# Sigmoid attention and gated layers on one core: half loads of the first group, four value loads per batch, another first pass

## The chip, the cores and the metric

The kernel runs on one core of a Trainium2 chip. A core has TensorE (matrix products into PSUM), VectorE, ScalarE, GpSimd and SyncE, each with its own instruction queue, worked off in order, and 16 DMA engines that all queues share. The metric is the time of one execution on the device, in microseconds; lower is better.

## The reference

The inputs are q, k, v of shape 8 x 12 x 448 x 64 (batches, heads, positions, width), two weights and a vector beta.

```python
scores = scale * np.matmul(q, k.transpose(0, 1, 3, 2)) - np.log(S)
attn = 1.0 / (1.0 + np.exp(-scores))
x = np.matmul(attn, v)                 # per head; then heads side by side: 3584 x 768
h = x @ w_in                           # 3584 x 2048
out = (h * (1.0 / (1.0 + np.exp(-beta * h)))) @ w_out    # 3584 x 768
```

There is no row sum in this attention, so a block of scores is finished after one sigmoid.

## The kernel before, in words

All matrix products are in fp16. A *group* is four heads of a batch, so a batch has three groups and there are 24 in all; a *pair* is two heads of a group. The tile `raws[g]` holds k and q of a group with 32 partitions per head: partition p of a head has positions 14p to 14p + 13, so that a load reads long rows. `transpose` turns them on VectorE in blocks of 32 x 32 into `kT` and `qT`, 32 partitions per head, whose two elements per position are the two halves of the head's width of 64.

`score` is one matmul with 32 rows: one head, one half of the width (`e`). Four heads of a group lie in four row groups of TensorE's array, and the loops put matmuls of different row groups next to each other. Keys are cut in four blocks: three of 128 and a last one of 64 (`KL`), of which two heads or pairs share a tile. Scores go into *score tiles* of two PSUM banks; in the first pass there are three of them (`share_psum(3)`), later two. `weigh` is ScalarE's sigmoid from a score tile into a slot of `attns`. `half_visit(g, c0, second)` makes the scores of a whole group for half of the queries (224): with `second` 0 the key blocks 0 and 1, with 1 the blocks 2 and the last. It takes two score tiles and gives two sigmoids, 128 x 896 each, or one of 896 and one of 448.

`attend` multiplies the weighted scores with v (432 matmuls on L340 in all) into one PSUM bank per pair, and VectorE casts the result to `xTs`. The values of a batch lie in `vs[b]`: block i of 32 partitions holds, per head, three key rows (`j` 0 to 2) and, in a fourth place (`JF`), the last 64 keys, which `double_v_last` copies from the lower 64 partitions to the upper on VectorE. `load_v_full` fills the first three places with four loads, `load_v_last` the fourth with two loads of short rows.

`dense1` is the first layer for a column block `dc` of 128 (six matmuls, then a sigmoid on ScalarE, L374, and a product on VectorE, L377); column blocks 2i and 2i + 1 need the w_in load `(2i, 2i + 2)`. Dense work is a list of *units* (one matmul each) that is poured between other work. Later batches use products with fewer multiplications (L531, L651), which the diff doesn't touch.

The order on each engine is the order of the code (a manual schedule). Loads into fp16 from fp32 are issued by GpSimd, in the order of `LOADS` for the start and `LATER` after it. The first group alone is loaded as fp32 by SyncE into `staged` and cast by ScalarE (`act` true, L806) and VectorE (L808). Then `BEGIN`, a list written by hand, gives the order of the first pass, that of batch 0: casts, transposes (`k`, `q` with a half of the queries), scores (`scores`, L237 and L250), values (`values`, L340), the copies of the last keys (`v`), dense units and `idle` matmuls on a tile of zeros (L822). An entry stands in the queue of whichever engines work on it, and an engine waits at its own part of it. After `BEGIN` come 74 *visits* (numbered from 0), each the scores of a group for one key block over all queries, with dense units behind it; how many follows from the work left over the visits left, and the tables `MORE` and `LATE` correct it by visit number.

Of the kernel before, what the change touches and what calls it, by code (L numbers as in the profile page):

```python
# [8 lines left out]
FP32 = mybir.dt.float32  # L9
FP16 = mybir.dt.float16  # L10
# [3 lines left out]
def kernel(  # L14
# [10 lines left out]
    nc = tc.nc  # L25
# [3 lines left out]
    B, H, S, D = q.shape  # L29
# [9 lines left out]
    NF = JF * P // BLK  # L39
# [103 lines left out]
    def load_v_full(b: int, lo: int = 0, hi: int = H):  # L143
# [4 lines left out]
        for i in range(HQ):  # L148
            nc.gpsimd.dma_start(
                out=vs[b][i * BLK : (i + 1) * BLK, lo:hi, 0:JF].rearrange("p h j d -> p h (j d)"),  # L150
                in_=rows[:, :, JF * i * D : JF * (i + 1) * D],
            )
            ready.update((b, "full", t, i) for t in range(lo // HQ, hi // HQ))

    def load_v_last(b: int):
        if b not in vs:
            vs[b] = vp.tile([P, H, JF + 1, D], FP16, tag="v16", name="v16")
        rows = v[b].rearrange("h (p c) d -> p h c d", c=NB)
        for c in range(NF, NB):
            lo = (c - NF) * BLK  # L160
            nc.gpsimd.dma_start(out=vs[b][lo : lo + BLK, :, JF], in_=rows[:, :, c])
        ready.add((b, "last"))

    def load_v(b: int):
        load_v_full(b)
        load_v_last(b)

    def double_v_last(b: int):
        assert (b, "last") in ready
        ready.add((b, "v"))  # L170
        nc.vector.tensor_copy(out=vs[b][KL:P, :, JF], in_=vs[b][0:KL, :, JF])
# [29 lines left out]
    def transpose(g: int, r: int, c0: int = 0, c1: int = NB):  # L201
        raw = raws[g][:, r]
        assert g or (r, c0) == (0, NB // 2) or all((r, "cast", c) in ready for c in range(c0, c1))
        if r == 0:
            if g not in qT:
                qT[g] = qTp.tile([P, NB * BLK, PAIR], FP16, tag="qT", name="qT")
            ready.update((g, "q", c) for c in range(c0, c1, NB // 2))
            nc.vector.transpose(
                out=in_order(g // QPB, qT[g][:, c0 * BLK : c1 * BLK]),
# [3 lines left out]
        ready.add((g, "k"))  # L213
        kT[g] = kTp.tile([P, S, PAIR], FP16, tag="kT", name="kT")
        to = kT[g].rearrange("p k e -> p (k e)").bitcast(FP32)
# [813 lines left out]
```

## Time and profile before

| | us |
|---|---|
| median of 3 runs (373.41 to 374.0) | 373.94 |
| profiled execution | 374.6 |
| its span | 372.8 |
| TensorE busy in it | 365.8 (98%) |
| ScalarE busy | 259.9 (70%) |
| VectorE busy | 254.5 (68%) |
| GpSimd busy | 90.6 (24%) |

In the rows of the profile PE is TensorE, PEld its weight loads, ACT ScalarE, DVE VectorE, POOL GpSimd; L340 is line 340 of the kernel. A row of a timeline gives start, length, engine, line, operation, output and inputs, shapes and how many, and in brackets the idle time of that engine just before it and what ended it. Matmuls of a few instructions are merged in one row; ends of matmuls are modelled. The granted clock is 1.00 in all parts of the span.

### The profile page before, as it was taken

The numbers are of one execution on the slowest core, as the hardware profiler recorded it, in microseconds if no ns is written. First come the engines' busy times: TensorE is split into PE (matmuls) and PEld (weight loads), VectorE is DVE, ScalarE is ACT, GpSimd is POOL, SyncE is SP. The second block draws the span as 40 slices with busy tenths as digits, with TensorE's granted clock in tenths as the row PEclk, the third lists the DMA queues.
The fourth block names the chain that finished last, engine by engine and source line by source line (L and its number), as shares of the span: only waits on it lengthen the run. The fifth ranks groups of instructions, "written<-read, shape, count | busy, mean of one in ns | idle before, by whom it ended". The sixth has DMA issues, their size and how long they took to land.

```text
span 372.8 us, 7320 instructions
## 1 busy us (share of the span) xinstructions
PE 365.8 (98%) x2906; PEld 184.4 (49%) x2906; DVE 254.5 (68%) x479; ACT 259.9 (70%) x311; POOL 90.6 (24%) x136
## 2 busy tenths in 40 slices
PE   7989999999999999999999999999999999999997
PEld 4566644443444455544444445554444455555655
DVE  3435696877496966787667666778667666669671
ACT  5995777699876658887777749887787647883000
POOL 6833253151151012325123003235100002230000
PEclk9999999999999999999999999999999999999999
DMA  9999999993359030039829511018903111000334
GB/s 162 165 189 202 197 203 201 245 125 51 49 76 183 2 86 1 0 51 125 157 42 206 108 26 33 3 17 116 172 6 86 42 44 42 1 2 1 86 84 128
DMA packets 42626, 34.65 MB, mean 93 GB/s; under 512 B 21968, under 2 KB 39008, under 8 KB 42592
## 3 DMA queue, kind: packets, MB, share of 16 engines
q0 software_dynamic: 36688, 22.47, 44.5%
q1 hardware_dynamic: 5904, 11.71, 11.1%
q8 instruction: 23, 0.38, 0.4%
q14 instruction: 11, 0.09, 0.1%
HBM read 45.62 MB, written 11.01 MB: 152 GB/s over the span
## 4 chain that ended last, share of the span: by engine, by line
PE 92%; ACT 5%; issue 1%; DMA 1%; DVE 1%; ACTq 0%
PE ps L651 27%; PE ps L531 26%; PE ps L237 11%; PE ps L340 10%; PE ps L362 9%; PE ps L392 4%; PE ps L445 4%; ACT attns L250 3%; DMA gt<-in_k_dram 1%; ACT attns L265 1%; ACT sg L374 1%; DVE gt L377 0%; DVE kT L217 0%; ACT raw L806 0%; ACT osb L672 0%
## 5 line engine op out<-in xcount | busy, mean ns | idle before, releaser
L265 ACT ACTIVATE attns<-ps,nlogs 128x1792 f16<-128x1792 f32 x75 | 131.6, 1755 | 41.7 <-PE ps L237 41.6
L651 PEld LDWEIGHTS <-sum 128*128 128x128 f16 x440 | 40.5, 98 | 37.3 <-issue 12.5
L545 POOL TENSOR_TENSOR gt<-attns,sg 128x448 f16<-128x448 f32 x21 | 23.9, 1139 | 141.7 <-ACT sg L542 141.7
L237 PE MATMUL ps<-qT,kT 32*128 32x448 f16 (+3 forms) x864 | 52.1, 339 | 1.2 <-ACT attns L250 0.4
L542 ACT ACTIVATE sg<-ps,beta_sb 128x448 f32<-128x448 f32 x72 | 45.2, 632 | 8.4 <-PE ps L531 5.9
L531 PE MATMUL ps<-xT,w_in 128*128 128x448 f16 x216 | 49.2, 353 | 0.0
L531 PE MATMUL ps<-xT,w_S 128*128 128x448 f16 x216 | 49.2, 352 | 0.0
L651 PE MATMUL ps<-w_T,sum 128*128 128x384 f16 x264 | 48.7, 327 | 0.0
L545 DVE TENSOR_TENSOR gt<-ps,sg 128x448 f16<-128x448 f32 x72 | 44.3, 618 | 4.0 <-ACT sg L542 3.8
L349 DVE CAST xT<-ps 128x448 f16<-128x448 f32 (+1 forms) x54 | 28.8, 567 | 21.0 <-PE ps L340 21.0
L531 PEld LDWEIGHTS <-w_in 128*128 128x128 f16 x288 | 28.0, 98 | 26.6 <-issue 0.7
L362 PE MATMUL ps<-xT,w_in 128*128 128x448 f16 (+1 forms) x240 | 39.9, 316 | 1.2 <-DMA w_in<-in_moe_w_in_dram 0.6
L340 PE MATMUL ps<-attns,v 128*64 128x448 f16 (+3 forms) x432 | 40.4, 340 | 0.6 <-issue 0.6
L669 DVE TENSOR_TENSOR osb<-ps,osb 128x384 f32<-128x384 f32 x55 | 30.5, 554 | 15.1 <-PE ps L651 12.8
L638 DVE TENSOR_TENSOR sum<-gt 128x1024 f16<-128x1024 f16 x55 | 36.5, 678 | 0.2
L377 DVE TENSOR_TENSOR gt<-ps,sg 128x448 f16<-128x448 f32 (+1 forms) x40 | 20.1, 527 | 23.2 <-ACT sg L374 23.1
L126 POOL DMA_DIRECT2D raw<-in_q_dram x26 | 14.5, 559 | 79.6 <-DVE kT L221 72.6
L651 PE MATMUL ps<-w_out,gt 128*128 128x384 f16 x176 | 33.3, 327 | 0.0
L651 PE MATMUL ps<-w_out,sum 128*128 128x384 f16 x176 | 32.3, 327 | 0.0
L591 DVE TENSOR_TENSOR ps<-ps,attns 128x448 f32<-128x448 f32 x24 | 15.2, 632 | 23.3 <-PE ps L531 19.3
L362 PEld LDWEIGHTS <-w_in 128*128 128x128 f16 x240 | 21.8, 98 | 18.0 <-issue 5.4
L531 PEld LDWEIGHTS <-w_S 128*128 128x128 f16 x216 | 21.1, 98 | 19.4
(54 smaller groups left out, 376.4 us busy)
## 6 DMA issues: line engine op xcount, KB each, us to landing
out_dram<-osb SPq DMA_DIRECT2D x100, 96.0 KB, 2.1
raw<-in_k_dram POOLq DMA_DIRECT2D x23, 224.0 KB, 5.5
raw<-in_q_dram POOLq DMA_DIRECT2D x21, 224.0 KB, 3.9
v<-in_v_dram POOLq DMA_DIRECT2D x32, 144.0 KB, 6.2
w_in<-in_moe_w_in_dram POOLq DMA_DIRECT2D x8, 384.0 KB, 11.8
w_out<-in_moe_w_out_dram POOLq DMA_DIRECT2D x4, 768.0 KB, 13.4
v<-in_v_dram POOLq DMA_DIRECT2D x16, 48.0 KB, 6.1
out_dram<-osb SPq DMA_DIRECT2D x5, 144.0 KB, 2.4
```

Of the source, the lines that this page charges most:

```text
L237: nc.tensor.matmul(sco[base : base + nk, hh, u0 : u0 + n], kT[g][lo : lo + BLK, jt * P : jt * P + nk, e], qT[g][lo : lo + BLK, c0 : c0 + n ...
L265: nc.scalar.activation(out=attns[:, slot : slot + 2].rearrange("p n h s -> p (n h) s"), in_=sco, func=AF.Sigmoid, bias=nlogs[:, 0:1], scal ...
L340: nc.tensor.matmul(av[hh * D : (hh + 1) * D, 0:n], vs[b][base : base + nk, 2 * (s % NPAIR) + hh, jt], at[base : base + nk, hh, 0:n], start ...
L349: nc.vector.tensor_copy(out=xTs[b][:, s % NPAIR, c0 : c0 + n], in_=av[:, 0:n])
L362: nc.tensor.matmul(m1, w_in16[:, hc, dc * P : (dc + 1) * P], xTs[b][:, hc, c0 : c0 + n], start=(hc == 0), stop=(hc == NHC - 1),)
L377: nc.vector.tensor_tensor(out=gt[:, dc, off : off + n], in0=m1, in1=sg[:, 0:n], op=ALU.mult)
L531: nc.tensor.matmul(out, w[:, c, i * P : (i + 1) * P], m[:, c], start=(start and c == 0), stop=(c == KH - 1), skip_group_check=not start,)
L542: nc.scalar.activation(out=sg, in_=h, func=AF.Sigmoid, bias=0.0, scale=beta_sb[:, dc : dc + 1])
L545: return lambda: engine.tensor_tensor(out=gt[:, dc, b % 2 * S : b % 2 * S + S], in0=h, in1=sg, op=ALU.mult)
L638: nc.vector.tensor_tensor(out=sums[t, i], in0=x, in1=y, op=op)
L651: nc.tensor.matmul(m2, (x if op is None else sums[t, i])[:, dc], w[:, dc], start=first, stop=(dc == ND - 1), skip_group_check=i >= 4,)
L669: nc.vector.tensor_tensor(out=out, in0=in0, in1=in1, op=op)
```

## The change

The first group's loads of k and q are cut by pairs of heads: four loads of 64 partitions instead of two of 128, and casts and transposes for each pair. A new `pair_visit` makes the scores of one pair for key blocks 0 and 1: one score tile, one sigmoid of 128 x 896. In `BEGIN` it stands for four of the half visits. The keys are dealt to the blocks differently, so that the last 64 keys belong to blocks 0 and 1 (`rows_of`: these hold four key rows per partition, blocks 2 and 3 three). A batch's values then come in four loads, two of them with rows a third longer, and the two loads of short rows fall away; `transpose` of k is cut in 256 and 192 columns instead of 384 and 64. Batch 0's values are loaded as those of group 0, ahead of group 2's q, and the rest after it; the copy of the last keys is cut likewise. Two memsets move from GpSimd to VectorE. `BEGIN` and two entries of `MORE` are new.

```diff
-    def load_v_full(b: int, lo: int = 0, hi: int = H):
+    def rows_of(i: int):
+        n = JF + int(i < KL // BLK)
+        return i * JF + min(i, KL // BLK), n
+
+    def load_v(b: int, lo: int = 0, hi: int = H):
...
         for i in range(HQ):
+            c, n = rows_of(i)
             nc.gpsimd.dma_start(
-                out=vs[b][i * BLK : (i + 1) * BLK, lo:hi, 0:JF].rearrange("p h j d -> p h (j d)"),
-                in_=rows[:, :, JF * i * D : JF * (i + 1) * D],
+                out=vs[b][i * BLK : (i + 1) * BLK, lo:hi, 0:n].rearrange("p h j d -> p h (j d)"),
+                in_=rows[:, :, c * D : (c + n) * D],
             )
-    def load_v_last(b: int):
...
-    def double_v_last(b: int):
-        nc.vector.tensor_copy(out=vs[b][KL:P, :, JF], in_=vs[b][0:KL, :, JF])
+    def double_v_last(b: int, lo: int = 0, hi: int = QPB):
+        heads = slice(lo * HQ, hi * HQ)
+        nc.vector.tensor_copy(out=vs[b][KL:P, heads, JF], in_=vs[b][0:KL, heads, JF])
...
-        nc.vector.transpose(
-            out=to[:, 0 : JF * P].rearrange("p (j i q) -> p i j q", j=JF, i=HQ),
-            in_=frm[:, 0:NF].rearrange("p (i j) f -> p i j f", j=JF),
-        )
-        nc.vector.transpose(
-            out=to[:, JF * P :], in_=frm[:, NF:].rearrange("p c f -> p (c f)")
-        )
+        half = to.rearrange("p (x i q) -> p x i q", i=2, q=BLK)
+        for i in (0, 2):
+            c, n = rows_of(i)
+            nc.vector.transpose(
+                out=half[:, i // 2 :: 2].rearrange("p j i q -> p i j q"),
+                in_=frm[:, c : c + 2 * n].rearrange("p (i j) f -> p i j f", j=n),
+            )
...
+    def pair_visit(g: int, c0: int, x: int):
+        s, sco = 2 * g + x, score_tile()
+        for jt in (0, 1):
+            for e in range(PAIR):
+                for hh in range(2):
+                    score(sco, jt * QH, s, jt, hh, e, c0, QH)
+        slot = weigh(sco, S)
...
         LOADS = [
-            ("q", 1, 0), ("k", 1), ("k", 2), ("last",), ("q", 2, 0), ("v", 0, 3), ("q", 1, 1), ("q", 0, 1),
-            ("q", 2, 1), ("w_in", 0, 2), ("w_in", 2, 4), ("w_in", 4, 6), ("w_in", 6, 8), ("w_in", 8, 10),
+            ("q", 1, 0), ("k", 1), ("k", 2), ("v", 0, 1), ("q", 2, 0), ("v", 1, 3), ("q", 0, 1), ("q", 2, 1),
+            ("q", 1, 1), ("w_in", 0, 2), ("w_in", 2, 4), ("w_in", 4, 6), ("w_in", 6, 8), ("w_in", 8, 10),
...
-        for r, (to, n) in parts.items():
-            nc.sync.dma_start(
-                out=to[:, 0 : n * D],
-                in_=(q, k)[r][0, 0:HQ].rearrange("h (p c) d -> (h p) (c d)", c=NB)[:, 0 : n * D],
-            )
+        for x in (0, 1):
+            rows = slice(x * 2 * BLK, (x + 1) * 2 * BLK)
+            for r, (to, n) in parts.items():
+                nc.sync.dma_start(
+                    out=to[rows, 0 : n * D],
+                    in_=(q, k)[r][0, 2 * x : 2 * (x + 1)].rearrange("h (p c) d -> (h p) (c d)", c=NB)[:, 0 : n * D],
+                )
...
-        nc.gpsimd.memset(nlogs, NEG_LOG_S)
-        nc.gpsimd.memset(dummy, 0.0)
...
+        nc.vector.memset(dummy, 0.0)
+        nc.vector.memset(nlogs, NEG_LOG_S)
...
         BEGIN = [
-            ("cast", 1, 0, 8, False), ("cast", 1, 8, 14, True), ("cast", 0, 0, 7, True), ("k", 0), ("q", 0, 0),
-            ("q", 1, 0), ("idle", 20), ("scores", 0, 0, 1), ("idle", 4), ("scores", 0, 0, 0), ("k", 1),
-            ("idle", 2), ("k", 2), ("q", 2, 0), ("idle", 2), ("scores", 1, 0, 0), ("beta",), ("idle", 8),
-            ("scores", 1, 0, 1), ("v", 0), ("idle", 6), ("scores", 2, 0, 0), ("values", 0, 0), ("q", 1, 1),
-            ("scores", 2, 0, 1), ("q", 0, 1), ("values", 1, 0), ("scores", 0, 1, 0),
-            ("values", 2, 0), ("scores", 0, 1, 1), ("dense", 12), ("scores", 1, 1, 1), ("two",), ("dense", 6),
-            ("scores", 1, 1, 0), ("loads",), ("q", 2, 1), ("dense", 21), ("scores", 2, 1, 0), ("dense", 9),
-            ("values", 0, 1), ("scores", 2, 1, 1), ("values", 1, 1), ("values", 2, 1), ("dense", 39), ("k", 3),
-            ("q", 3, 0), ("q", 3, 1), ("dense", 45),
+            ("cast", 1, 0, 0, 9, False), ("cast", 1, 0, 9, 14, True), ("cast", 0, 0, 0, 7, True), ("k", 0, 0),
+            ("q", 0, 0, 0), ("cast", 1, 1, 0, 7, False), ("cast", 1, 1, 7, 14, True),
+            ("cast", 0, 1, 0, 7, True), ("k", 0, 1), ("q", 0, 0, 1), ("idle", 17), ("pair", 0, 0, 0),
+            ("q", 1, 0), ("scores", 0, 0, 1), ("pair", 0, 0, 1), ("idle", 4), ("k", 1), ("idle", 2), ("k", 2),
+            ("v", 0, 1), ("q", 2, 0), ("pair", 1, 0, 0), ("pair", 1, 0, 1), ("idle", 2), ("values", 0, 0),
+            ("beta",), ("scores", 1, 0, 1), ("idle", 2), ("pair", 2, 0, 0), ("pair", 2, 0, 1), ("v", 1, 3),
+            ("q", 0, 1), ("q", 1, 1), ("values", 1, 0), ("scores", 2, 0, 1), ("pair", 0, 1, 0),
+            ("pair", 0, 1, 1), ("values", 2, 0), ("scores", 0, 1, 1), ("dense", 12), ("scores", 1, 1, 1),
+            ("two",), ("dense", 6), ("scores", 1, 1, 0), ("loads",), ("q", 2, 1), ("dense", 21),
+            ("scores", 2, 1, 0), ("dense", 9), ("values", 0, 1), ("scores", 2, 1, 1), ("values", 1, 1),
+            ("values", 2, 1), ("dense", 33), ("k", 3), ("q", 3, 1), ("q", 3, 0), ("dense", 45),
         ]
...
         MORE = {
-            0: -1, 2: 1, 3: -4, 8: -3, 9: 1, 10: 1, 12: 2, 13: 1, 14: -2, 15: 1, 16: -1, 17: -2, 19: -1, 20: -2,
+            0: -1, 2: 2, 3: -3, 8: -3, 9: 1, 10: 1, 12: 2, 13: 1, 14: -2, 15: 1, 16: -1, 17: -2, 19: -1, 20: -2,
...
-            54: 1, 59: 1, 62: 1, 67: -1,
+            54: 1, 59: 1, 62: 1, 67: -1, 80: 2, 82: 1,
```

More of the change, by code (lines that the diff above doesn't have):

```diff
@@ L232, in score @@
         g, lo = s // 2, (s % 2 * 2 + hh) * BLK
[L233 to L234 removed]
+        assert (g, "k", s % 2) in ready and all(
+            (g, "q", c, s % 2) in ready for c in range(c0 // BLK, (c0 + n) // BLK, NB // 2)
         )
```

64 lines of the change are left out of this document (28 added, 36 removed).

## The prediction

> **What bounds the kernel now.** I read the windows by stage first, then ScalarE's, TensorE's and the weight loads' timelines of the first 31 us, and last GpSimd's timeline with each load's time to landing. In the windows (columns: window and its length; busy time and instructions of TensorE, weight loads, VectorE, ScalarE, GpSimd; clock; DMA share; GB/s) TensorE is full from 31.2 us on. What the change rewrites lies ahead of that:
>
> ```profile
> 6.00:16.00 10.00, 8.68 (x142) 4.91 (x143) 4.23 (x14) 8.82 (x11) 7.12 (x12) 1.00 1.35 169
> 16.00:31.20 15.20, 13.91 (x222) 9.30 (x216) 6.35 (x19) 13.86 (x20) 6.53 (x9) 1.00 1.41 186
> 31.20:44.00 12.80, 12.80 (x92) 8.18 (x92) 8.00 (x19) 7.01 (x14) 3.00 (x5) 1.00 1.33 202
> 44.00:74.00 30.00, 30.00 (x272) 13.69 (x265) 23.15 (x40) 21.45 (x15) 11.40 (x19) 1.00 1.29 215
> ```
>
> Much of TensorE's time before 31 us is idle matmuls and waiting; ScalarE is the full engine there. Its timeline (start, length, then the idle before it) shows the first sigmoid of the scores at 6.70, and hardly a gap from there to 24:
>
> ```profile
> 4.35 1.10 ACT L806 CAST raw<-gt 128x384 f16<-128x384 f32 x2 [2.11 <-DMA gt<-in_k_dram]
> 6.70 8.68 ACT L250 ACTIVATE attns<-ps,nlogs 128x896 f16<-128x896 f32 x10 [1.25 <-PE ps L237]
> 15.75 4.99 ACT L250 ACTIVATE attns<-ps,nlogs 128x896 f16<-128x896 f32 x6 [0.37 <-PE ps L237]
> 23.04 1.79 ACT L265 ACTIVATE attns<-ps,nlogs 128x1792 f16<-128x1792 f32 x1
> 26.62 1.75 ACT L265 ACTIVATE attns<-ps,nlogs 128x1792 f16<-128x1792 f32 x1 [0.57 <-PE ps L237]
> ```
>
> The weight loads of TensorE, one engine further on, show what the whole start waits for: at 14.05 the values, and at 24.24 and 25.59 the third and fourth load of w_in.
>
> ```profile
> 14.05 0.55 PEld L340 LDWEIGHTS <-v 128*64 128x64 f16 x12 [0.80 <-DMA v<-in_v_dram]
> ...
> 24.24 1.07 PEld L362 LDWEIGHTS <-w_in 128*128 128x128 f16 x12 [0.87 <-DMA w_in<-in_moe_w_in_dram]
> 25.59 0.21 PEld L362 LDWEIGHTS <-w_in 128*128 128x128 f16 x3 [0.28 <-DMA w_in<-in_moe_w_in_dram]
> ```
>
> Issue plus time to landing gives the loads in microseconds from the start: k of group 1 8.3, k of group 2 9.5, the two `last` loads of v 10.5 and 10.8, group 2's q 11.3, the four big v loads 11.7 to 14.0 (0.75 apart), the late halves of q 14.6 to 15.7, then w_in 18.9, 21.0, 24.2, 25.55. GpSimd issues all of these:
>
> ```profile
> 8.56 0.61 POOL L149 DMA_DIRECT2D v<-in_v_dram  x1 [1.19 <-DMA raw<-in_k_dram]
> 9.80 0.56 POOL L126 DMA_DIRECT2D raw<-in_q_dram  x1 [0.63 <-DMA raw<-in_k_dram]
> 10.78 1.07 POOL L126 DMA_DIRECT2D raw<-in_q_dram  x2 [0.42 <-DMA v<-in_v_dram]
> 11.84 6.59 POOL L177 DMA_DIRECT2D w_in<-in_moe_w_in_dram  x8
> ```
>
> From the ninth on, each issue waits for the landing of the load eight before it.
>
> **The change, step by step.** Times are starts from the profiled execution, 374.6 us (span 372.8, 1.8 around it); the median of the runs is 373.94, 0.66 lower, and I take the same difference off both.
>
> *First score.* All of k lands at 4.32, q's half at 4.86. Half the rows land somewhere between half of k's 3.58 us after 0.74 (2.5) and no earlier than now (4.3); I take 3.2 for k and 3.6 for q, nearer to the early end because 448 KB and 224 KB are moved one after the other now, and 4.5 and 4.9 for the second half, whose last byte cannot come earlier. Casts: no row has a cast over 64 partitions; it costs between half and all of one over 128, and I take all, since an engine goes through the columns. So by 0.51 us for 384 columns and 0.57 for 448, ScalarE's four cost 0.43 + 3 x 0.57 instead of 1.08, one microsecond more. VectorE's cast (0.48), kT's two transposes (0.50 + 0.13 now for 448 columns; 0.64 for 256 + 192) and qT (0.37) follow the first landing to 4.8; the 17 idle matmuls end at 4.95 (20 take 4.45). So the first pair's scores begin near 4.95 instead of 5.94. ScalarE must first do the second half's casts, queued ahead of its sigmoid: 4.52, 5.07, then the first sigmoid at 5.6 instead of 6.70. Gain 1.1.
>
> *Where that goes.* The second half's transposes end at 6.2, the next scores need all four heads (0.75 to the sigmoid, as 5.94 to 6.70 now), so the second sigmoid stands at 7.0 and ScalarE idles 0.5. Group 0's first half is then done by 9.3 (0.91 per sigmoid, 0.52 for a narrow one); k of group 1 lands at 8.3, its transposes take 0.64, a pair's scores about 0.55: next sigmoid 9.6 instead of 10.1. Gain 0.45. No row shows a pair's eight matmuls, which use two row groups and not four. Bounds: 0.35 (half of sixteen) and 0.8 (the slower sixteen, 0.75); I take 0.55, near the fast sixteen's 0.51. At 0.8 the start still ends with its wait for w_in; only at 1.0 would the start be longer than now, by 0.8.
>
> *Values earlier.* `values` of group 0 moves ahead of the scores of (1, 0, 1) on TensorE's queue. Its four small loads follow k of group 2 (9.5). They are a third of 4 x 0.75 = 3.0, plus the bytes of `last`, so 1.2: landed at 10.7. TensorE waits 0.3, runs 0.92, and the scores behind it reach ScalarE at 12.4 instead of 11.9: it idles about one microsecond. Loss 0.5. It is given back where `values` stood (the gap before 15.75, and 0.16 after each narrow sigmoid, which a pair's single score tile removes): (2, 0, 1) at 15.7 instead of 15.75, the first two-tile sigmoid at 22.8 instead of 23.04. ScalarE's chain is thus 0.2 ahead, and without any wait for weights TensorE would reach the last `values` of the start 0.86 earlier than now. The second value load (two groups) and its copy, 0.42 now and 0.2 + 0.3 after in two pieces, lie on VectorE, 42% busy there.
>
> *The weights.* Dense columns 4 to 7 need the third and fourth w_in loads, and nothing behind them in TensorE's order is changed until the visits. So the gain of the start is what the fourth landing (25.55) gains, at most 0.86. Bytes ahead of it are the same. GpSimd loses two memsets: 0.07 (they start 0.035 apart) to 0.55 (0.74 to 1.29, when the first load is issued), and I take 0.07, as the 0.42 behind them are not theirs. The two `last` loads bring 96 KB in 1.29 us; in the big loads' pace, 144 KB in 0.75, these bytes need 0.50, so 0 to 0.79 are saved; I take 0.25, as the queue is seldom held up by one kind of load. Against it, fifteen loads and not thirteen stand before w_in on GpSimd at about 0.6 each: with the same eight-load wait, I get the first w_in issue at 12.65 instead of 11.84, a cost of 0 (the q loads ahead of it land until 15) to 0.8; I take 0, since w_in lands 7.1 us after its issue, most of it queueing. Sum: 0.07 + 0.25 = 0.3 earlier; ends 1.3 earlier (of which 0.86 count) and 0.8 later.
>
> The Trainium skill, "DMA: Bandwidth & Descriptors", section Specifications, says that an element below 512 B costs a read-modify-write. By that rule the loads that now bring 512 B a row would run faster than the old 384 B and the gain would be the whole 0.86. The trace disagrees for 384 B: 144 KB per 0.75 us is the pace of w_in's 512 B pieces (384 KB per 2.0 us); only the 128 B pieces of `last` are slower.
>
> *After 31 us.* Six dense units move from ahead of the first visit into the visits; TensorE is full on both sides, so 0, with 0.3 either way for the order. Every k is transposed in 256 + 192 columns instead of 384 + 64: same elements, same count, 0. Two value loads less per batch are 1.3 us of GpSimd (24% busy) per batch: 0; were GpSimd late, the next k and q would gain. The entries 80 and 82 of the unit table have no visit (74 there are): 0.
>
> Sum: -0.3, so 374.3 for a profiled execution, 373.6 for the median.
>
> **Rivals.** A difference within 0.2% (0.75 us) can hardly be told from none.
> (1) *The fourth w_in load pins the start*, as above: 373.6, its own range 373.2 to 374.4. Speaking for it: the 0.87 and 0.28 waits. If half loads land no earlier than whole ones, the change doesn't do what it says at 4.95, yet this case stays, because k of group 1 and the values bind next.
> (2) *The weights come early enough*, 0.8 or more: the start ends when ScalarE lets it, 0.86 earlier, 373.1; with 0.3 from the order of the visits 372.8. For it: the slow 128 B loads vanish. Against: bytes are the same, and w_in's own pace of 2.0 us does not change.
> (3) *The weights come later*, slower: two more issues ahead of w_in push its first issue by 0.8; as soon as the fourth lands after 25.55, each further microsecond is one on the span: 374.7 at the full 0.8. For it: GpSimd is 71% busy from 6 to 16 us. Against: 7.1 us from issue to landing. The values' wait can't do this before they land 0.9 late.
>
> **Numbers.** Case 1 has 0.48, case 2 0.27, case 3 0.25 (it includes visits that fit worse by some 0.5 after the move). These are also the chances of same, faster, slower. Prediction 373.6. The range takes in most of cases 2 and 3: 372.7 to 375.0.
>
> **What would show it.** First sigmoid near 5.6; a ScalarE gap of about 1 us before 12.4; `values` near 10.75; weight loads still waiting for w_in around 25.3; span up to 31 us shorter by 0.3. Wrong, if no weight load waits for w_in (case 2), if the fourth w_in lands after 25.55 (case 3), if a pair's scores take 1.0, or if TensorE shows new gaps after 40 us.

## The result, and the profile after

The changed kernel takes 378.42 us (median of 6 runs, 377.52 to 380.64) where the kernel before takes 373.97 (6 runs beside them, 373.41 to 374.69): 1.0126 times as long, 95% interval 1.0098 to 1.0155. The prediction was 373.6 with a range to 375.0, so the result lies outside it, and the loss is 4.5 us.

The profiled execution took 378.47 us, its span is 376.7, 3.9 above the 372.8 of before. The windows of the changed kernel, cut as before (window and length; busy time of TensorE, weight loads, VectorE, ScalarE, GpSimd; clock; DMA share; GB/s):

```profile
6.00:16.00 10.00, 6.32 (x68) 3.51 (x67) 4.03 (x12) 5.98 (x8) 6.58 (x11) 0.66 1.10 150
16.00:31.20 15.20, 13.85 (x224) 9.34 (x222) 6.41 (x20) 14.54 (x21) 7.93 (x11) 1.00 1.39 186
31.20:44.00 12.80, 12.65 (x126) 8.15 (x121) 7.93 (x21) 7.81 (x14) 2.96 (x6) 1.00 1.31 203
44.00:74.00 30.00, 30.00 (x262) 14.67 (x259) 21.79 (x38) 21.51 (x18) 9.11 (x15) 1.00 1.18 192
```

Between 6 and 16 us ScalarE does 5.98 us of work where it did 8.82, and the granted clock of TensorE, 1.00 before, is 0.66. Everything from 31 us on is the work of before, moved by a constant: the last block of TensorE starts at 368.31 instead of 364.82, 3.49 later, and the two-tile sigmoids in between are 3.36 to 3.49 later all the way from 56 us. Another 0.4 came with the landing of the last stores. So the loss was made in the first 31 us.

ScalarE's timeline of the changed kernel shows where (start, length, engine and line, and in brackets the idle time just before, with what ended it):

```profile
4.32 0.46 ACT L815 CAST raw<-gt 64x320 f16<-64x320 f32 x1 [2.09 <-DMA gt<-in_k_dram]
5.17 0.56 ACT L815 CAST raw<-gt 64x448 f16<-64x448 f32 x1 [0.39 <-DMA gt<-in_q_dram]
8.44 0.56 ACT L815 CAST raw<-gt 64x448 f16<-64x448 f32 x1 [2.71 <-DMA gt<-in_k_dram]
9.30 0.56 ACT L815 CAST raw<-gt 64x448 f16<-64x448 f32 x1 [0.29 <-DMA gt<-in_q_dram]
9.88 1.01 ACT L247 ACTIVATE attns<-ps,nlogs 128x896 f16<-128x896 f32 x1
...
17.14 8.06 ACT L247 ACTIVATE attns<-ps,nlogs 128x896 f16<-128x896 f32 x10 [0.66 <-PE ps L234]
```

The first half of k is there at 4.3, no earlier than all of k before (4.32), the first half of q at 5.14, later than q before (4.86). The second halves land at 8.4 and 9.3. The first sigmoid, at 6.70 before, starts at 9.88 behind their casts. TensorE's timeline has the same hole, 3.46 us without a matmul:

```profile
6.22 0.67 PE L234 MATMUL ps<-qT,kT 32*128 32x224 f16 x10 [1.22 <-DVE qT L204]
10.35 1.93 PE L234 MATMUL ps<-qT,kT 32*128 32x224 f16 x22 [3.46 <-DVE qT L204]
```

SyncE issues the four halves one after the other, 0.57 to 0.60 us each (before: 0.38 and 0.42), so the last is issued at 2.62, while GpSimd has issued loads since 1.24. The chain that ended last begins with exactly this load:

```profile
2.62 6.65 DMA gt<-in_q_dram
9.28 0.02 issue
9.30 0.57 ACT raw L815
9.87 0.02 issue
9.89 0.42 DVE qT L204
10.31 0.04 issue
10.35 1.93 PE ps L234 x21
```

GpSimd's timeline of the changed kernel, to be held against the one shown in the prediction:

```profile
9.38 0.58 POOL L154 DMA_DIRECT2D v<-in_v_dram  x1 [2.82 <-DMA raw<-in_k_dram]
10.55 1.15 POOL L154 DMA_DIRECT2D v<-in_v_dram  x2 [0.60 <-DMA raw<-in_k_dram]
11.69 1.65 POOL L125 DMA_DIRECT2D raw<-in_q_dram  x3
13.31 0.86 POOL L171 DMA_DIRECT2D w_in<-in_moe_w_in_dram  x1
```

Its wait for k of group 1 is 2.82 instead of 1.19, and the first w_in load is issued at 13.31 instead of 11.84; yet no weight load of TensorE waits for w_in any more, since everything ahead of it is later still.

### The profile page after: what moved, and what is told of

It is laid out like the page before. It is cut to its first block, busy times and chain, and to the rows that moved or that the text cites. A ratio compares the mean times of both kernels' runs of the same rounds, so it can differ in the third digit from the quotient of the medians.

```text
span 376.7 us, 7285 instructions
## 1 busy us (share of the span) xinstructions
PE 366.0 (97%) x2891; PEld 184.6 (49%) x2891; DVE 256.3 (68%) x486; ACT 260.6 (69%) x313; POOL 82.9 (22%) x122
## 4 chain that ended last, share of the span: by engine, by line
PE 91%; ACT 5%; DMA 2%; issue 1%; SPq 0%; DVE 0%; ACTq 0%
PE ps L659 27%; PE ps L539 25%; PE ps L234 11%; PE ps L348 10%; PE ps L370 9%; PE ps L400 4%; PE ps L453 4%; ACT attns L247 3%; DMA gt<-in_q_dram 2%; ACT attns L262 1%; ACT sg L382 1%; PE ps L831 1%; SPq L805 0%; DVE gt L385 0%; ACT raw L815 0%
## 5 line engine op out<-in xcount | busy, mean ns | idle before, releaser
L234 PE MATMUL ps<-qT,kT 32*128 32x448 f16 (+3 forms) x864 | 53.4, 344 | 5.6 <-DVE qT L204 4.7
L539 PEld LDWEIGHTS <-w_in 128*128 128x128 f16 x288 | 28.0, 98 | 26.6 <-issue 0.7
L234 PEld LDWEIGHTS <-kT 32*128 32x128 f16 (+1 forms) x864 | 15.6, 97 | 33.8 <-issue 28.1
```

What stands on the lines that cost most here:

```text
L234: nc.tensor.matmul(sco[base : base + nk, hh, u0 : u0 + n], kT[g][lo : lo + BLK, jt * P : jt * P + nk, e], qT[g][lo : lo + BLK, c0 : c0 + n ...
L539: nc.tensor.matmul(out, w[:, c, i * P : (i + 1) * P], m[:, c], start=(start and c == 0), stop=(c == KH - 1), skip_group_check=not start,)
```

## Experiments on the half loads

All times below are medians; each interval is the ratio to runs of the kernel before on the same chip (373.2 to 373.7 there).

**The half loads undone, and the half loads alone.** The first kernel is the changed one with two whole loads by SyncE; casts and transposes stay by pairs.

```diff
-        for x in (0, 1):
-            rows = slice(x * 2 * BLK, (x + 1) * 2 * BLK)
-            for r, (to, n) in parts.items():
-                nc.sync.dma_start(
-                    out=to[rows, 0 : n * D],
-                    in_=(q, k)[r][0, 2 * x : 2 * (x + 1)].rearrange("h (p c) d -> (h p) (c d)", c=NB)[:, 0 : n * D],
-                )
+        for r, (to, n) in parts.items():
+            nc.sync.dma_start(
+                out=to[:, 0 : n * D],
+                in_=(q, k)[r][0, 0:HQ].rearrange("h (p c) d -> (h p) (c d)", c=NB)[:, 0 : n * D],
+            )
```

> The changed kernel with the first group's k and q loaded whole again (two loads of 128 partitions); casts, transposes, pairs, values and order stay as changed. Theory A (the second half loads arrive late, at 8.4 and 9.3 us, because four short loads begin later and then share the DMA engines with GpSimd's loads; all of the 3.5 us lost up to 31 us comes from there): k lands near 4.3, q near 4.9, first sigmoid near 6.5, no long TensorE gap, clock 1.00, 373.4 to 374.3. Theory B (pairs on two row groups and the new order of the first pass cost the time): still above 376.5.

Measured: 374.93, ratio 1.0036 (1.0020 to 1.0052), between the ranges of the two theories and nearer to the first. The second kernel is the one before, with only its two loads cut in four (the same diff the other way round, on that kernel):

> The kernel before with only the first group's k and q loads cut in half loads, in the changed kernel's order; its casts still need both halves. Theory A: the last half of k lands near 8.4, the last half of q near 9.3, the first sigmoid moves from 6.7 to about 11, and the time rises by about 4 to 378. Theory B: within 0.75 of before.

Measured: 378.86, ratio 1.0139 (1.0120 to 1.0157), the whole loss and a little more; the first sigmoid there is at 10.99. The second halves of k and q land at 6.8 and 8.8 there, earlier than in the changed kernel, whose GpSimd issues other loads behind k of group 2. So the half loads are worth 3.5 us in the changed kernel (378.42 less 374.93), and what is left with whole loads stands some 1.2 behind the kernel before. The two prices don't add: the cut alone cost 5.1 us.

**Why the second half is late.** In one kernel the second halves are issued by ScalarE, so that they don't stand behind the first ones in SyncE's queue.

```diff
-                nc.sync.dma_start(
+                (nc.sync, nc.scalar)[x].dma_start(
```

> The changed kernel with the second pair's two half loads issued from ScalarE's queue instead of SyncE's. If the second halves are late because they are issued third and fourth on one queue (0.62 apart) and start only when the queue gets to them: they land before 6, first sigmoid near 6.5, time 373.6 to 375. If they are late because GpSimd's loads take the DMA engines from 3 us on, whoever issues: they land at 7 or later and the time stays above 377.

Measured: 376.55, ratio 1.0076 (1.0061 to 1.0091). All halves land by 6.9 us, and the first sigmoid starts at 8.16; this lies between the two cases that were expected. In another, GpSimd's loads are held back:

```diff
+        hold = const.tile([P, 128], FP32, name="hold")
+        for _ in range(14):
+            nc.gpsimd.memset(hold, 0.0)
         for x in LOADS:
             load(*x)
```

> The changed kernel, with fourteen memsets of a scratch tile on GpSimd ahead of its first load, so that its loads start some 2 us later. Theory A1, sharing: the second halves are late because GpSimd's k of groups 1 and 2 move at the same time; then they land here at about 5.8 (k) and 6.9 (q) instead of 8.4 and 9.3, although everything of GpSimd lands 1 to 2 us later, and the time is within 1 us of the changed kernel. Theory A2, a half load is slow by itself (64 partitions use part of the engines): k still lands at 7.5 or later and the time is 379.5 or more.

Measured: 377.20 (376.50 to 380.18), ratio 1.0113 (1.0083 to 1.0143). GpSimd's first load was issued at 4.28 instead of 1.24. ScalarE's timeline of this kernel:

```profile
4.19 1.13 ACT L815 CAST raw<-gt 64x320 f16<-64x320 f32 x2 [1.96 <-DMA gt<-in_k_dram]
5.83 1.13 ACT L815 CAST raw<-gt 64x448 f16<-64x448 f32 x2 [0.51 <-DMA gt<-in_k_dram]
6.98 1.01 ACT L247 ACTIVATE attns<-ps,nlogs 128x896 f16<-128x896 f32 x1
```

The casts of the second half start at 5.83 instead of 8.44 (8.23 and 8.48 in two kernels further on with the same loads), with the same four issues by SyncE at the same times. So of the lateness of the second k, 2.6 us is the sharing of the DMA engines with GpSimd's loads, which were issued before it; without that it lands 1.5 us behind the whole load, which is about what the two additional issues ahead of it take (2 x 0.6). That a load over 64 partitions is slow by itself, the other theory, does not fit: with only the half loads under way they moved 363 GB/s here (last column), where the kernel before reaches at most 376 GB/s in 0.4 us windows of its first loads.

```profile
2.80:3.20 0.40, 0.40 (x4) 0.28 (x3) 0.00 (x0) 0.00 (x0) 0.31 (x2) 1.00 1.00 363
```

The time gained only 1.2. The first two-tile sigmoid came 3.0 earlier (24.51 instead of 27.50), but the first w_in load was issued no earlier (13.34 and 13.31), and TensorE waited 0.76 us for w_in at 27.00. Moving the issue to ScalarE may have helped in the same way: the halves were issued earlier, so that less of GpSimd's traffic stands ahead of them. That kernel doesn't separate the two.

The Trainium skill has this as a rule: "DMA: Bandwidth & Descriptors", section Rules for kernel authors, advises against two transfers to disjoint partition halves, because both use all the DMA engines and so follow each other, and for one transfer of 128 partitions. The runs agree (1.0139 for the cut alone); of the 4.1 us by which the second half of k is later than the whole load here, 2.6 come from the loads of the other queue.

**The order behind it.** The first pair's scores were done at 6.9, but its sigmoid stood behind the second half's casts in ScalarE's queue. This kernel puts those casts and transposes behind the first pair in `BEGIN`.

```diff
-            ("q", 0, 0, 0), ("cast", 1, 1, 0, 7, False), ("cast", 1, 1, 7, 14, True),
-            ("cast", 0, 1, 0, 7, True), ("k", 0, 1), ("q", 0, 0, 1), ("idle", 17), ("pair", 0, 0, 0),
+            ("q", 0, 0, 0), ("idle", 17), ("pair", 0, 0, 0), ("cast", 1, 1, 0, 7, False), ("cast", 1, 1, 7, 14, True),
+            ("cast", 0, 1, 0, 7, True), ("k", 0, 1), ("q", 0, 0, 1),
```

> The changed kernel with the second half's casts and transposes behind the first pair's scores and sigmoid in the program. The first sigmoid then starts at about 7 instead of 9.88. Theory I, the queue order costs: one sigmoid of 0.9 is out of the way when the second pair's scores come, and the time falls by 0.5 to 0.9, to 377.5 to 377.9. Theory J, the second pair's scores bind: the next sigmoid starts at 11.1 to 11.5 as now, the gap behind the first is just longer, and the time stays at 378.1 to 378.7.

Measured: 378.83 (378.56 to 379.44), ratio 1.0154 (1.0137 to 1.0171): nothing gained. The first sigmoid starts at 7.18, and the next one still at 11.50 (11.48 in the changed kernel), released by the second pair's scores. The landing binds, not the queue.

**The clock.** TensorE's hole may have a second price. Windows of the changed kernel, same columns:

```profile
5.75:9.10 3.35, 0.67 (x10) 0.41 (x9) 0.86 (x3) 0.56 (x1) 0.81 (x2) 1.00 1.19 195
9.15:15.95 6.80, 5.60 (x56) 3.08 (x58) 3.36 (x10) 5.37 (x7) 5.97 (x10) 0.50 1.06 131
16.05:20.00 3.95, 3.72 (x70) 2.02 (x70) 2.80 (x10) 3.29 (x5) 3.86 (x5) 1.00 1.28 167
```

After 3.4 us with 0.67 us of matmuls the granted clock is 0.50 for 6.8 us. This kernel keeps TensorE busy there.

```diff
-("idle", 17), ("pair", 0, 0, 0),
+("idle", 17), ("pair", 0, 0, 0), ("idle", 30),
```

> The changed kernel with 30 more idle matmuls behind the first pair's scores, which fill TensorE's wait of 3.46 us before 10.35. Theory A with the half clock from 9.2 to 16.0 as a part of the loss: clock 1.00, second scores still near 10.35, and about 0.7 to 1.2 us won (TensorE's rows between 10.35 and 16 are that much longer than at full clock): 377.2 to 377.8. If the clock costs nothing because the loads set the pace: 378.4 as changed, within 0.4.

Measured: 377.43 (376.41 to 378.35), ratio 1.0091 (1.0067 to 1.0115), 1 us less than the changed kernel, although the thirty idle matmuls took 4.89 us and held the second pair's scores back to 11.98 instead of 10.35. So about 1 us of the loss may be the half clock's; the two intervals overlap, so this is not clear of noise. "TensorE: Matmul & The Clock Gate", Part 1 of the Trainium skill, names half rate after an idle window of about 3.4 us; the three windows above agree with it.

The column with the clock has to be read beside the lengths of the matmuls. The kernel with the other order of casts has the same hole, and its column says 1.00 in the same window:

```profile
9.15:15.95 6.80, 5.57 (x56) 3.06 (x58) 3.25 (x10) 4.34 (x6) 5.91 (x10) 1.00 1.09 125
12.24 1.46 PE L831 MATMUL ps<-still 128*128 128x256 f16 x6
```

But the six idle matmuls take 1.46 us there, as in the changed kernel at 12.22 with the clock at 0.50; in the kernel before the same six take 0.83 (at 11.76). They take 1.46 also in the kernel with ScalarE's issues and in the one with GpSimd held back, both with 1.00 in the column. Slow matmuls stand under 1.00 at the start of the changed kernel as well: 17 idle ones in 3.81 us, 224 ns each, against 138 ns for the six in the kernel before. In the kernel with the other order, the first ten score matmuls take 1.12 us, where they take 0.67 in the changed kernel. So its TensorE seems not to have reached full pace at all before about 16 us, and that it gained nothing over the changed kernel is no sign that the pace is free.

## Experiments on the rest of the change

**The clock with whole loads.** With whole loads the clock was still 0.50 from 7.9 to 14.7 us, and the first theory for the remaining 1.2 us was this.

```diff
-("idle", 17), ("pair", 0, 0, 0),
+("idle", 22), ("pair", 0, 0, 0), ("idle", 6),
```

> Loads of group 0 whole, all else as changed, and idle matmuls put in: 22 instead of 17 ahead of the first pair, 6 behind it. Theory C, the half clock: with whole loads TensorE had too little work between 4.5 and 7.9 us and ran at the half clock until 14.7 us, and that is the 1.2 us by which that kernel still stood behind the one before. Then the clock here stays full, the three gaps of ScalarE (1.07, 0.67 and 1.23 us) shrink to about 0.4 each, and the time comes to 373.5 to 374.1. Theory B, the order of pairs and values: the clock is full but the gaps ahead of the group-1 pairs and behind the values stay, 374.6 to 375.0.

Measured: 374.97 (374.09 to 375.30), ratio 1.0033 (1.0021 to 1.0045), the same as without the idle matmuls. Both theories fell. The clock was full, six idle matmuls took 0.83 us, and ScalarE's gaps were closed:

```profile
6.97 1.01 ACT L247 ACTIVATE attns<-ps,nlogs 128x896 f16<-128x896 f32 x1 [0.58 <-PE ps L234]
8.37 12.18 ACT L247 ACTIVATE attns<-ps,nlogs 128x896 f16<-128x896 f32 x15 [0.40 <-PE ps L234]
```

The first two-tile sigmoid came at 22.86 (25.29 without the idle matmuls, in an execution of 375.95, 1.0 above that kernel's median), and it didn't shorten the time: TensorE then waited four times for w_in between 19 and 25.5 us (0.2 to 1.0 each), and once for w_out:

```profile
60.33 0.65 PE L400 MATMUL ps<-w_out,gt 128*128 128x384 f16 x3 [0.44 <-DMA w_out<-in_moe_w_out_dram]
```

So behind ScalarE's chain stands a second bound, the stream of loads. Two more kernels followed from it. In one the values of group 0 stand further back, behind group 2's pairs:

```diff
-("idle", 2), ("values", 0, 0), ("beta",), ("scores", 1, 0, 1), ("idle", 2), ("pair", 2, 0, 0), ("pair", 2, 0, 1),
+("idle", 2), ("beta",), ("scores", 1, 0, 1), ("idle", 2), ("pair", 2, 0, 0), ("pair", 2, 0, 1), ("values", 0, 0),
```

> As the kernel with whole loads and idle matmuls, but the values of group 0's first half stand behind group 2's pair scores instead of ahead of group 1's third score. Theory B: the values wait for their load at 10.1 and for the double copy and hold TensorE while ScalarE has nothing; moved back, ScalarE's gap ahead of that score closes (0.5 to 1.2 us less at the start) and the time is 0.3 to 0.8 below the kernel with idle matmuls. Theory C: with the full clock the values cost 1.0 us either way, and what ends the start is the landing of the weights, so the two are within 0.3.

Measured: 376.67, with a spread of 374.70 to 379.78, ratio 1.0098 (1.0060 to 1.0136). Theory B fell: put there, group 0's and group 1's values follow each other, and ScalarE has a gap of 1.38 us ahead of 17.11. The four executions at a mean clock of 0.98 to 0.99 took 378.0 to 379.8, the four at 1.00 took 374.7 to 375.4. In the other the later w_out loads go ahead of group 5's k and q:

```diff
-("values", 1), ("qk", 4), ("qk", 5), ("w_out", 0, 1), ("w_out", 1, 1),
+("values", 1), ("qk", 4), ("w_out", 0, 1), ("w_out", 1, 1), ("qk", 5),
```

> As the kernel with whole loads and idle matmuls (374.97), but the two later w_out loads stand ahead of group 5's loads in GpSimd's queue. There the start was 0.37 ahead of the profiled kernel before at 56 us and 0.36 behind at 71 us, and TensorE waited 0.44 us at 60.3 us for w_out. Theory F, the load stream is a second bound behind the start: w_out lands about 2 us earlier, the wait is gone, and the time falls by 0.5 to 0.8, to 374.2 to 374.5. If the wait was not what set the end, the time stays at 374.8 to 375.1; if group 5's loads become late instead, 375.5 or more.

Measured: 375.65 (375.01 to 376.83), ratio 1.0054 (1.0034 to 1.0074). The wait for w_out is gone, and group 5's loads are late instead, as the last of the three expectations has it. VectorE waits 5.90 us for group 5's q until 58.70, and the transposes of its k come behind that:

```profile
61.65 0.59 PE L234 MATMUL ps<-qT,kT 32*64 32x448 f16 x12 [1.33 <-DVE kT L217]
```

In this order, what is moved ahead makes another load late; other orders weren't tried.

**Memsets alone.** This kernel is the one before with the two memsets on VectorE.

```diff
-        nc.gpsimd.memset(nlogs, NEG_LOG_S)
-        nc.gpsimd.memset(dummy, 0.0)
...
         nc.vector.memset(beta_in, 0.0)
+        nc.vector.memset(dummy, 0.0)
+        nc.vector.memset(nlogs, NEG_LOG_S)
```

> The kernel before with one edit: the memsets of nlogs and dummy on VectorE instead of GpSimd. The prediction's term: 0.07 earlier on GpSimd's queue, so 373.4 to 373.9 against 373.55 to 373.7 of before, within 0.2%. If the first issue of GpSimd (1.29 us before) moving by 0.06 changed how the first loads share the engines, k of group 1 would land more than 0.3 earlier or later than 8.27 and the time would move by as much.

Measured: 373.33 against 373.32, ratio 0.9995 (0.9986 to 1.0005): nothing. But its profile is of use as a second look at what is nearly the kernel before, in an execution of 371.2 us span instead of 372.8. ScalarE:

```profile
3.93 1.11 ACT L806 CAST raw<-gt 128x384 f16<-128x384 f32 x2 [1.70 <-DMA gt<-in_k_dram]
6.42 13.56 ACT L250 ACTIVATE attns<-ps,nlogs 128x896 f16<-128x896 f32 x16 [1.39 <-PE ps L237]
```

GpSimd:

```profile
7.84 0.61 POOL L149 DMA_DIRECT2D v<-in_v_dram  x1 [1.19 <-DMA raw<-in_k_dram]
8.95 1.72 POOL L126 DMA_DIRECT2D raw<-in_q_dram  x3 [0.50 <-DMA raw<-in_k_dram]
10.65 3.31 POOL L177 DMA_DIRECT2D w_in<-in_moe_w_in_dram  x4
```

Sixteen sigmoids without a gap, the first w_in load issued at 10.65 instead of 11.84, the four landings at 16.9, 19.0, 21.0 and 23.7 instead of 18.9 to 25.55, and no wait of TensorE for w_in at all. GpSimd's first load had landed at 5.6 instead of 6.5, and each issue from the ninth on follows the landing of the load eight before it. So the profile that the prediction was worked out from was of an execution with a late first load; in this one ScalarE's chain is the bound, and w_in has a little slack. The memsets don't decide it: the kernel with the values further back has them on VectorE too, and there GpSimd waits 1.20 us for its first load. Which kind is the usual one is not shown, as this execution lies 0.4 below its kernel's median and the profiled one of before lies 0.66 above.

**The value loads.** This kernel has the memsets on VectorE, the four-load values with their order, and the transposes of k by 256 and 192 columns; the first group's loads, casts, idle matmuls and scores are as before. A first version had the copy of the last keys of groups 1 and 2 behind the transpose of q (0, 1) on VectorE, this study's own edit:

```diff
-("scores", 2, 0, 0), ("values", 0, 0), ("q", 1, 1), ("scores", 2, 0, 1), ("q", 0, 1), ("values", 1, 0),
+("scores", 2, 0, 0), ("values", 0, 0), ("q", 0, 1), ("v", 1, 3), ("scores", 2, 0, 1), ("q", 1, 1), ("values", 1, 0),
```

> Only the memsets on VectorE, the value loads by four, their order and the two transposes by halves of k: group 0's loads, casts, idle matmuls and scores are those of the kernel before, by whole groups. If what is left over after the halves lies in the clock or in the order of pairs (theories B and C), this kernel shows none of it: fourth w_in pair at 25.2 to 25.5 (25.55 before) and 373.4 to 373.9, as the prediction's term of 0.3 less has it. If the loads' new order costs (theory D), 374.5 or more.

Measured: 374.89 (373.89 to 376.27), ratio 1.0038 (1.0025 to 1.0050); TensorE waited 1.38 us for that copy, until 17.19. With the copy ahead, as the change has it:

```diff
-("values", 0, 0), ("q", 0, 1), ("v", 1, 3),
+("values", 0, 0), ("v", 1, 3), ("q", 0, 1),
```

> As the kernel with the value loads, memsets and transposes alone, but the double copy of groups 1 and 2's values stands on VectorE ahead of the transposes of q (0,1) and (1,1), as the change has it. In the run before, TensorE waited 1.38 us at 17.2 for that copy, which stood behind a transpose whose load landed at 16.4; that is this study's own edit. Without it the prediction's term for the loads (0.3 earlier) asks for 373.3 to 373.8; theory D, the new order of loads costs by itself, for 374.4 or more.

Measured: 374.76 (374.19 to 376.41), ratio 1.0037 (1.0023 to 1.0051): theory D. Its GpSimd rows, and the weight loads of TensorE:

```profile
7.89 0.58 POOL L154 DMA_DIRECT2D v<-in_v_dram  x1 [1.23 <-DMA raw<-in_k_dram]
9.22 1.14 POOL L154 DMA_DIRECT2D v<-in_v_dram  x2 [0.76 <-DMA raw<-in_k_dram]
10.35 1.65 POOL L125 DMA_DIRECT2D raw<-in_q_dram  x3
11.96 1.70 POOL L171 DMA_DIRECT2D w_in<-in_moe_w_in_dram  x2
```

```profile
19.16 1.07 PEld L370 LDWEIGHTS <-w_in 128*128 128x128 f16 x12 [0.95 <-DMA w_in<-in_moe_w_in_dram]
25.20 0.21 PEld L370 LDWEIGHTS <-w_in 128*128 128x128 f16 x3 [0.82 <-DMA w_in<-in_moe_w_in_dram]
```

The wait for k of group 1 ends at the same place as in the kernel with the memsets (7.89 and 7.84), but then two more issues stand ahead of w_in, 1.3 us later at 11.96, and TensorE waits for w_in again.

**Issues alone.** To hold this against the shape of the loads, one kernel adds to the one before only two loads of 256 bytes ahead of the first w_in load.

```diff
-            ("q", 2, 1), ("w_in", 0, 2),
+            ("q", 2, 1), ("small", 0), ("small", 1), ("w_in", 0, 2),
```

> The kernel before plus two loads of 256 bytes on GpSimd ahead of the first w_in load: two more issues, no data to speak of. Theory G: from about 9 us on the loads follow GpSimd's issues (a load of q landed 4.6 us after its issue in the kernels with memsets or loads alone), so two more issues of 0.42 to 0.6 move the first w_in issue from 10.65 to about 11.7 and its landing from 16.9 to 18.5 or 19, and the time rises by 0.8 to 1.4, to 374.2 to 374.8. If the weights have slack, or the value loads by four are slow by their shape, 373.3 to 373.6.

Measured: 374.31 (373.81 to 374.84) where the 29 runs of before beside it have a median of 373.52; the ratio of 1.0013 (1.0002 to 1.0024) is nearer to none, as some of those runs reach 375.47. The trace does not show the two issues as what costs: the first w_in load was issued at 12.92, 1.1 later than in the profile before, but landed at 18.2, 0.7 earlier than there. TensorE's longest wait is for the values, whose loads stand ahead of the two small ones:

```profile
14.57 0.99 PE L340 MATMUL ps<-attns,v 128*64 128x224 f16 x16 [1.12 <-DMA v<-in_v_dram]
25.45 0.46 PE L362 MATMUL ps<-xT,w_in 128*128 128x224 f16 x3 [0.18 <-DMA w_in<-in_moe_w_in_dram]
```

This too is an execution with a late first load, 372.7 us of span where the one before has 372.8. The other kernel takes issues away: batch 0's values in four loads instead of eight, and the late halves of q in the order of before. Behind it in `BEGIN`, the copy of the last keys is in one piece again and stands further back; all else is as in the kernel with the value loads.

```diff
-            ("q", 1, 0), ("k", 1), ("k", 2), ("v", 0, 1), ("q", 2, 0), ("v", 1, 3), ("q", 0, 1), ("q", 2, 1),
-            ("q", 1, 1), ("w_in", 0, 2),
+            ("q", 1, 0), ("k", 1), ("k", 2), ("q", 2, 0), ("v", 0, 3), ("q", 1, 1), ("q", 0, 1), ("q", 2, 1),
+            ("w_in", 0, 2),
```

> As the kernel with the value loads alone (374.76), but batch 0's values come in four loads in all instead of four for group 0 and four for the rest: two issues fewer than before, four fewer than changed. Theory G: first w_in issue at about 9.5 to 10, landing at 16 to 16.9, and the time is that of before or a little less, 372.9 to 373.6; values of group 0 may wait for the last of the four, up to 0.4 of that given back. If the loads by four or the transposes by halves of k cost by themselves, 374.4 or more.

Measured: 373.43 (373.28 to 374.44), ratio 0.9995 (0.9983 to 1.0006): level with before. So neither value loads by four nor the new transposes of k cost anything by themselves. What costs came with the four additional issues and their order; the four issues are the likeliest, since TensorE waits for w_in with them (above) and not without, but the order changed along with them. GpSimd and ScalarE of this kernel:

```profile
9.39 0.53 POOL L125 DMA_DIRECT2D raw<-in_q_dram  x1 [0.67 <-DMA raw<-in_k_dram]
10.20 4.12 POOL L171 DMA_DIRECT2D w_in<-in_moe_w_in_dram  x5 [0.28 <-DMA raw<-in_q_dram]
```

```profile
6.71 13.57 ACT L247 ACTIVATE attns<-ps,nlogs 128x896 f16<-128x896 f32 x16 [1.25 <-PE ps L234]
```

**Holding GpSimd back with whole loads.** Three memsets ahead of its first load in the last kernel:

```diff
+        for _ in range(3):
+            nc.gpsimd.memset(hold, 0.0)
         for x in LOADS:
```

> The kernel with whole loads, group 0 as before and batch 0's values in four loads (373.43), with GpSimd's first load held back by three memsets (about 0.6 us). Theory A1 carried on to whole loads: with less sharing k and q of group 0 land at 3.9 and 4.4 instead of 4.3 and 4.9, the first sigmoid comes 0.3 earlier, and the chain of sigmoids carries it: 373.0 to 373.3. If whole loads are through before GpSimd's move, nothing is gained at the front and k of group 1 lands 0.6 later (8.5 instead of 7.9): 373.4 to 374.0.

Measured: 373.78 (373.15 to 374.07), ratio 1.0000 (0.9989 to 1.0012). This told little: the memsets ran in time that GpSimd had been idle, and its first load was issued at 1.41 instead of 1.23. k and q landed at 4.2 and 4.8.

**Pairs with the value loads of before.** The pairs, whole loads and idle matmuls, with six value loads for batch 0 and the order of loads of before; the values of group 0 then stand behind group 2's pairs. Beside the functions for the values and the transposes of k, taken from the kernel before, and the place of the values, the edit to the kernel with the idle matmuls is:

```diff
-            ("q", 1, 0), ("k", 1), ("k", 2), ("v", 0, 1), ("q", 2, 0), ("v", 1, 3), ("q", 0, 1), ("q", 2, 1),
-            ("q", 1, 1), ("w_in", 0, 2),
+            ("q", 1, 0), ("k", 1), ("k", 2), ("last",), ("q", 2, 0), ("v", 0, 3), ("q", 1, 1), ("q", 0, 1),
+            ("q", 2, 1), ("w_in", 0, 2),
```

> The pairs with whole loads of group 0, idle matmuls for the clock, and the value loads and the order of loads of before (six issues for values). Theory G: the weights are as early as before, and what is left is the price of the pairs: casts of group 0 over 64 partitions at twice the number (2.15 instead of 1.11 us on ScalarE), which put the second sigmoid at 8.4 and the chain of sigmoids 0.5 behind; 373.6 to 374.1. Theory H, the pairs cost the 1.4 us: 374.6 or more.

Measured: 375.27, with a spread of 374.71 to 379.58, ratio 1.0076 (1.0044 to 1.0109). As in the kernel with the values further back there are two kinds of executions: five at a mean clock of 0.98 to 0.99 (378.1 to 379.6, the profiled one among them), seven at 1.00 (374.7 to 375.3). Windows of the profiled one:

```profile
6.90:13.50 6.60, 5.75 (x82) 3.12 (x81) 3.73 (x14) 6.13 (x8) 5.22 (x8) 1.00 1.50 186
13.70:20.30 6.60, 5.88 (x64) 3.31 (x61) 1.99 (x6) 3.17 (x5) 4.51 (x7) 0.50 1.45 197
```

Here the lengths agree with the column: sixteen value matmuls take 1.66 us at 14.39, where they take 0.99 at full pace, and the clock is 0.50 until about 27 us.

Theory H is nearer by the numbers, but the kernel doesn't settle it, because the place of the values, which cost a gap of 1.38 in the other kernel with that order, came with it. What pairs cost by themselves lies between 0.2 us (374.97 with pairs and idle matmuls against 374.76 without pairs, both with the late weights) and 1.4 us here (374.9, the median of the seven at a full clock, against 373.5; 1.8 with all twelve) and stays open. Part of it can be read: group 0's casts on ScalarE take 2.15 instead of 1.11 us, as a cast over 64 partitions (0.56 for 448 columns) takes as long as one over 128, and the chain of sigmoids begins at 8.37 after a single one, where it begins at 6.2 to 7.0 without pairs.

No kernel beat the one before.

## Why the prediction was wrong

**First score.** The step that failed is the landing of the second half, "4.5 and 4.9 for the second half, whose last byte cannot come earlier". That is a lower bound, and it was used as the value; an upper bound wasn't given. Measured: 8.4 and 9.3. Two things were left out of it: each half is an issue of 0.6 on SyncE, and GpSimd's loads, issued from 1.24 on, share the DMA engines. With these loads held back, the second k landed at 5.8 and not at 8.4, and the second q at 6.4 and not at 9.3. The first halves were mis-sized too, 3.2 and 3.6 against 4.3 and 5.14: at the late end of the bounds, and beyond it. Casts over 64 partitions (all of the price of 128, 0.46 and 0.56 measured) and the eight matmuls of a pair (0.55; measured 0.57 at full pace) came out as predicted, and the queueing of the sigmoid behind the casts was seen rightly. The first sigmoid stood at 9.88 instead of 5.6.

**The rival that should have caught it** said that the case stays if half loads land no earlier than whole ones, because k of group 1 and the values bind next. It considered halves as late as whole loads, not later ones. With the second q at 9.3 group 0 itself binds, ahead of k of group 1, which became late too (9.1 instead of 8.3, and 8.1 at most with whole loads), since the halves share the engines in the other direction as well. The pace of TensorE wasn't in the prediction at all; the idle matmuls in `BEGIN`, and their reduction from 20 to 17, were read as filling only.

**Values earlier.** Seen with whole loads and full clock: the values of group 0 start at 10.78 (predicted 10.75), their load lands at 10.0 (10.7). The gap of a microsecond in ScalarE didn't come; its fifteen sigmoids have none.

**The weights.** Two errors. The fourth w_in load as the end of the start belongs to some executions and not to all: the kernel that differs by the memsets alone runs at the same time, and its profile has no such wait. And the two more issues ahead of w_in, 0 to 0.8 with 0 taken, were too cheap: the kernel with the value loads alone cost 1.4 us (374.76 against 373.32). That rival 3 had 374.7 for this mechanism is near by luck, as its cost of 0.8 stood on a time before that was 0.6 higher. The reason given for 0, that w_in is 7.1 us under way and mostly queues, doesn't hold for this kernel: its first w_in load was issued 1.3 later than in the kernel with the memsets alone and landed 2.2 later. The 0.25 gained from the short rows of `last` was not to be seen. Adding two tiny issues to the kernel before cost 0.5 (by the ratio) to 0.8 (by the medians), without a later landing of w_in than in the profile before; what makes up the 1.4, beyond that it goes away with four issues and their order, stays open. In the changed kernel itself no weight load waits, so there this error is hidden behind the first.

**After 31 us.** 0 within 0.3: right, the shift stays at 3.4 to 3.5.

Of the 4.5 us, then, 3.5 go away with whole loads. The last 1.0 (1.2 against the runs of before beside the kernel with whole loads) is not assigned: with whole loads ScalarE's chain came late in one profile, without a wait for w_in, and with its gaps closed the weights came late, and the time stayed the same. The prices of single parts can't be added up, as each hides the others.

## What to carry to other kernels

Before a load is cut to have its first part sooner, write down for each part when it is issued and what other queues have issued by then: the last part can land later by more than the first gains, and work that needs all parts then starts later. Where issues of one queue wait for the landing of earlier ones, count the issues as well as the bytes: two more value loads ahead of the weights went with 1.4 us here, and four fewer took it away. And if the profiled execution is off the median, see whether a wait in it belongs to the kernel or to that execution before a sum is put on it.

## What the runs showed of the hardware

- A load over 64 partitions took longer to issue on SyncE than one over 128, 0.57 to 0.60 against 0.38 to 0.42 us. The partitions alone don't explain it, as the unchanged load of beta behind them grew from 0.42 to 0.58 too. The first half of k (4.30) landed no earlier than all of k (4.32); why, stays open.
- In the changed kernel the granted clock fell to 0.50 after one stretch of 3.4 us with little TensorE work, and stayed there for 6.8 us, although TensorE was busy through 5.60 of them.
- The clock can fall in some executions of a kernel and not in others: with 5.75 us of matmuls in the 6.60 us before, it fell to 0.50 in the execution shown, and the times of that kernel lie in two heaps 4 us apart. What decides it wasn't found.
- The column with the clock can say 1.00 while matmuls take as long as at 0.50: six idle ones took 1.46 us with 0.50 and with 1.00 in it, and 0.83 at full pace.
